# Decode attention on one core: weights loaded per head group, q projected in pairs, PV matmuls packed two rows at a time

## The chip, the cores and the metric

One core of one Trainium2 chip. The metric is the device time of one execution in microseconds (us). Each number for a version is the median of several executions. A ratio is computed from rounds in which two kernels ran on the same chip: the mean time of one kernel's runs over the mean time of the other's in the same rounds, so it is not quite the ratio of the medians quoted beside it.

## The reference, cut to what matters

Two attention blocks, each for one new token of two sequences, with 32 heads of 192 and a cache of 8192 keys and values per head. Everything is bf16.

```python
q = (x @ wq).reshape(B, 1, 32, 192).transpose(0, 2, 1, 3)      # B = 2, x is (2, 1, 640)
scores = einsum("bhqd,bhkd->bhqk", q, k_cache) * 192 ** -0.5    # k_cache (2, 32, 8192, 192)
p = softmax(scores, axis=-1)
o = einsum("bhqk,bhkd->bhqd", p, v_cache)
return o.transpose(0, 2, 1, 3).reshape(B, 1, 32 * 192) @ wo     # wo (6144, 640)
# two such blocks, A and B, side by side in the output: (2, 1, 1280)
```

2 blocks x 32 heads x 2 sequences make 128 units. A unit reads 3.1 MB of K and 3.1 MB of V; with one query per head, nothing is read twice.

## The kernel before: the parts that matter

In a unit u, K lies as 128 partitions x 64 rows x 192 (T = 64). VectorE multiplies K by q; for the first NA = 30 rows ScalarE sums the products (one ACTIVATE with an accumulator per row), for the other 34 VectorE adds them up. The row maximum mp is reduced over the partitions by GpSimd (`mg`), GpSimd multiplies it by minus the scale (`nb`), ScalarE takes exp with nb as bias, and PE multiplies the probabilities with V.

```python
K1 = min(cfg.get("K1", 6), NA - 1)       # accumulations of unit u ahead of exp of unit u-1
NV = cfg.get("NV", 3)                    # buffers for V; K has NK = 2

# SyncE, in this order: every transfer of a unit
for u in range(NU):
    if u % B == 0: sp_head_loads(u // B)                       # wq, wo of one head
    S_sp.add(sp_k(u), waits=[key("d1b", u - NK)])
    if u >= 1:
        S_sp.add(sp_v(u - 1), waits=[key("pv", u - 1 - NV)])

# GpSimd: for each unit an all-reduce over the partitions, then the small nb
for u in range(NU):
    S_pool.add(pool_ar(u), waits=[key("d3", u), key("nb", u - 2)], sig=("ar", u))
    S_pool.add(pool_nb(u), waits=[("ar", u), key("exp", u - 2)], sig=("nb", u))

# VectorE, slot u
d1a(u)      # prodA = K[:, 0:30] * q           waits for K, for a0 (q ready), for accumulations of u-2
d3(u - 1)   # mp = max of the scores of u-1    waits for the last accumulation of u-1
d1b(u)      # prodD = K[:, 30:64] * q
l1, l2, l3, r(u)   # sums of prodD
# f2 (reciprocal) in odd slots

# ScalarE, slot u
for t in range(K1): act_acc(u, t)
act_exp(u - 1)                                   # waits for nb(u-1)
# f1, f4 (evictions of PV) in odd slots
act_a0(u + 1)                                    # q of u+1 from PSUM
for t in range(K1, NA): act_acc(u, t)

# PE, unit u: 64 matmuls of 192 columns
for t in range(T):
    eng.matmul(ops[0:1, b, 0:Dh], pb[u % 2][:, t:t + 1], vb[u % NV][:, t, :], start=(t == 0), stop=False)
```

## Time and profile before

| | before |
|---|---|
| median | 3093.31 us at first, 3094.33 us with the 16 runs of the comparison |
| per unit | about 24.0 us |
| busy: PE, VectorE, ScalarE, GpSimd | 36%, 47%, 46%, 15% |
| transfers | 271 GB/s mean, 67.6% of the queues' time |
| nb to mp (ScalarE's part of the loop) | 9.48 us |
| mp to nb (GpSimd's part) | 14.54 us |

Such numbers are read like this: no engine and no queue is full, so some chain of waits sets the pace. The prediction shows the chain.

```profile
POOL mg L213 <- issue: 73.8, 7, 10.7
```

### The profile page before, as it was taken

The numbers are of one execution on the slowest core, as the hardware profiler recorded it, in microseconds if no ns is written. First come the engines' busy times: TensorE is split into PE (matmuls) and PEld (weight loads), VectorE is DVE, ScalarE is ACT, GpSimd is POOL, SyncE is SP. The second block draws the span as 40 slices with busy tenths as digits, with TensorE's granted clock in tenths as the row PEclk, the third lists the DMA queues.
The fourth block names the chain that finished last, engine by engine and source line by source line (L and its number), as shares of the span: only waits on it lengthen the run. The fifth ranks groups of instructions, "written<-read, shape, count | busy, mean of one in ns | idle before, by whom it ended". The sixth has DMA issues, their size and how long they took to land.

```text
span 3097.1 us, 31016 instructions
## 1 busy us (share of the span) xinstructions
PE 1128.4 (36%) x9856; PEld 952.3 (31%) x9856; DVE 1455.4 (47%) x960; ACT 1439.4 (46%) x8195; POOL 465.3 (15%) x266
## 2 busy tenths in 40 slices
PE   2334333433334333433333433343334333343334
PEld 1223322332223322332223322333223322333223
DVE  4444454444444454444544454445444454445443
ACT  4445544544445444444444544454444444454444
POOL 1111111111111111111111111111111111111111
PEclk8666666666666666666666666666666666666666
DMA  9677677766676667766677667766676666766661
GB/s 380 273 295 288 252 279 284 284 257 262 274 284 277 257 268 290 282 257 257 272 286 281 259 263 283 283 273 262 269 295 272 257 272 269 291 265 262 278 262 79
DMA packets 94964, 838.78 MB, mean 271 GB/s; under 512 B 49736, under 2 KB 62032, under 8 KB 62032
## 3 DMA queue, kind: packets, MB, share of 16 engines
q1 hardware_dynamic: 94784, 836.79, 67.6%
q8 instruction: 78, 1.28, 0.2%
q14 instruction: 86, 0.70, 0.1%
q10 hardware_dynamic: 16, 0.01, 0.0%
HBM read 836.77 MB, written 0.01 MB: 270 GB/s over the span
## 4 chain that ended last, share of the span: by engine, by line
issue 82%; POOL 15%; POOLq 1%; ACT 1%; DMA 0%; PE 0%; DVE 0%; SPq 0%
POOL mg L213 14%; POOL nb L218 1%; ACT prodA L278 1%; DMA kb<-in_A_k_cache_dram 0%; POOLq L218 0%; PE ops L354 0%; POOLq L401 0%; DVE prodD L235 0%; DVE prodA L230 0%; POOLq L213 0%; POOLq L46 0%; SPq L145 0%; SPq L151 0%; DVE s L244 0%; PE oTps L362 0%
## 5 line engine op out<-in xcount | busy, mean ns | idle before, releaser
L354 PE MATMUL ops<-vb,pb 128*1 128x192 bf16 x8192 | 971.6, 298 | 1944.4 <-ACT pb L284 989.4
L354 PEld LDWEIGHTS ops<-vb,pb 128*1 128x1 bf16 x8192 | 822.3, 102 | 2092.1 <-ACT pb L284 1004.4
L278 ACT ACTIVATE prodA<-prodA 128x192 bf16<-128x192 bf16 x3840 | 1326.0, 347 | 12.2 <-DVE prodA L230 11.3
L284 ACT ACTIVATE pb<-sc,nb 128x64 bf16<-128x64 f32 x128 | 44.5, 348 | 1624.2 <-POOL nb L218 1624.2
L278 ACT ACTIVATION_READ_ACCUMULATOR prodA<-prodA 128x1 f32 x3840 | 718.7, 187 | 0.0
L230 DVE TENSOR_TENSOR prodA<-kb,qbc 128x5760 bf16<-128x5760 bf16 x128 | 404.3, 3159 | 499.0 <-ACT qbc L296 481.7
L213 POOL PARTITION_ALL_REDUCE mg<-mp x128 | 428.8, 3350 | 1264.0 <-DVE mp L240 1180.2
L235 DVE TENSOR_TENSOR prodD<-kb,qbc 128x6528 bf16<-128x6528 bf16 x128 | 454.2, 3549 | 0.0
L240 DVE TENSOR_REDUCE mp<-sc 128x1 f32<-128x64 f32 x128 | 28.2, 220 | 644.6 <-ACT prodA L278 644.6
L244 DVE TENSOR_TENSOR s<-prodD 128x3264 bf16<-128x3264 bf16 x128 | 237.8, 1858 | 4.4
L218 POOL TENSOR_SCALAR nb<-mg 128x1 f32<-128x1 f32 x128 | 33.4, 261 | 1347.9 <-issue 1347.9
L258 DVE RECIPROCAL rc<-o_sb 1x2 f32<-1x2 f32 x64 | 9.8, 154 | 475.7 <-ACT o_sb L289 475.7
L247 DVE TENSOR_TENSOR s<-s 128x1632 bf16<-128x1632 bf16 x128 | 129.0, 1008 | 4.4
L254 DVE TENSOR_REDUCE sc<-s 128x34 f32<-128x816 bf16 x128 | 128.4, 1003 | 4.4
L345 PE MATMUL qps<-wqs,xbc 128*128 128x192 bf16 x640 | 76.2, 251 | 21.0 <-ACT qbc L296 12.8
L250 DVE TENSOR_TENSOR s<-s 128x816 bf16<-128x816 bf16 x128 | 74.6, 583 | 4.4
L345 PEld LDWEIGHTS qps<-wqs,xbc 128*128 128x128 bf16 x640 | 47.0, 98 | 39.7 <-issue 33.3
L362 PE MATMUL oTps<-rc,o_sb 1*96 1x1 f32 x512 | 53.4, 221 | 0.0
L362 PEld LDWEIGHTS oTps<-rc,o_sb 1*96 1x96 f32 x512 | 48.0, 159 | 2.4 <-issue 0.3
L372 PE MATMUL outps<-wos,oTz 96*4 96x320 bf16 x256 | 45.0, 297 | 0.9 <-ACT oTz L292 0.9
L296 ACT ACTIVATE qbc<-qps 128x192 bf16<-128x192 f32 x128 | 39.2, 306 | 7.2 <-PE qps L345 7.2
L289 ACT ACTIVATE o_sb<-ops 1x386 f32<-1x386 f32 x64 | 29.9, 466 | 9.1 <-PE oTps L362 9.1
(14 smaller groups left out, 102.0 us busy)
## 6 DMA issues: line engine op xcount, KB each, us to landing
kb<-in_A_k_cache_dram SPq DMA_DIRECT2D x64, 3072.0 KB, 10.2
vb<-in_A_v_cache_dram SPq DMA_DIRECT2D x64, 3072.0 KB, 17.3
kb<-in_B_k_cache_dram SPq DMA_DIRECT2D x64, 3072.0 KB, 10.3
vb<-in_B_v_cache_dram SPq DMA_DIRECT2D x64, 3072.0 KB, 17.3
wqs<-in_A_wq_dram SPq DMA_DIRECT2D x32, 240.0 KB, 3.2
wos<-in_A_wo_dram SPq DMA_DIRECT2D x32, 240.0 KB, 3.5
wqs<-in_B_wq_dram SPq DMA_DIRECT2D x32, 240.0 KB, 3.3
wos<-in_B_wo_dram SPq DMA_DIRECT2D x32, 240.0 KB, 3.5
```

Of the source, the lines that this page charges most:

```text
L213: return eng.partition_all_reduce(mg[u % 2][:], mp[u % 2][:], 128, bass.bass_isa.ReduceOp.max)
L218: return eng.tensor_scalar(nb[u % 2][:], mg[u % 2][:], -scale, None, ALU.mult)
L230: return eng.tensor_tensor(prodA[u % 2][:], kb[u % NK][:, 0:NA, :], qb_bc(u, NA), ALU.mult)
L235: return eng.tensor_tensor(prodD[:], kb[u % NK][:, NA:T, :], qb_bc(u, ND), ALU.mult)
L244: return eng.tensor_tensor(s1[:], prodD[:, :, 0:96], prodD[:, :, 96:192], ALU.add)
L247: return eng.tensor_tensor(s2[:], s1[:, :, 0:48], s1[:, :, 48:96], ALU.add)
L250: return eng.tensor_tensor(s3[:], s2[:, :, 0:24], s2[:, :, 24:48], ALU.add)
L254: return eng.tensor_reduce(sc[u % 2][:, NA:T], s3[:], AXL.X, ALU.add)
L278: return eng.activation(prodA[u % 2][:, t, :], prodA[u % 2][:, t, :], ACTF.Identity, accum_out=sc[u % 2][:, t:t + 1])
L345: ins = eng.matmul(qps[:, 0:Dh], xbc[blk][b][:, c, :], wqs[g % NWQ][:, c, :], start=(c == 0), stop=(c == DC - 1))
L354: eng.matmul(ops[0:1, b, 0:Dh], pb[u % 2][:, t:t + 1], vb[u % NV][:, t, :], start=(t == 0), stop=False)
L362: ins = eng.matmul(oTps[0:HP, 2 * c + b:2 * c + b + 1], o_sb[0:1, b, HP * c:HP * (c + 1)], rc[0:1, b, :], start=True, stop=True)
```

## The change

The intent: fewer, longer weight loads (four heads at once), one q projection for two heads, half as many PV matmuls with twice the columns, in-place additions that free memory, and the first use of the activation table moved to the start. With it come two numbers that the short description does not name: K1 from 6 to 18, and V's buffers from three to two.

```diff
-    K1 = min(cfg.get("K1", 6), NA - 1)
+    K1 = min(cfg.get("K1", 18), NA - 1)
-    NV = cfg.get("NV", 3)
+    NV = cfg.get("NV", 2)
+    HG = cfg.get("HG", 4)
 ...
-        pb = [sb(f"pb{i}", [128, T], BF16) for i in range(2)]
+        pb = [sb(f"pb{i}", [128, T // 2, 33], BF16) for i in range(2)]      # columns 0 and 32 used, rest 0
-        wqs = [sb(f"wqs{i}", [128, DC, Dh], BF16) for i in range(NWQ)]
-        wos = [sb(f"wos{i}", [HP, 2, D], BF16) for i in range(NWO)]
+        wqs = [sb(f"wqs{i}", [128, DC, HG * Dh], BF16) for i in range(2)]
+        wos = [sb(f"wos{i}", [HP, HG, 2, D], BF16) for i in range(2)]
 ...
-        for blk in range(NBLK):
-            for b in range(B):
-                S_sp.add(sp_x(blk, b))
+        for b in range(B):
+            S_sp.add(sp_x(0, b))
+        S_sp.add(sp_wq(0))
         for u in range(NU):
-            if u % B == 0:
-                sp_head_loads(u // B)
+            if u % UG == 0: ...                      # wq of the next group, wo of this one
             S_sp.add(sp_k(u), waits=[key("d1b", u - NK)])
             if u >= 1:
                 S_sp.add(sp_v(u - 1), waits=[key("pv", u - 1 - NV)])
+            if u == 1:
+                for blk in range(1, NBLK):
+                    for b in range(B):
+                        S_sp.add(sp_x(blk, b))
 ...
         def act_f1(eng):
-            return eng.activation(o_sb[:], ops[0:1, :, 0:Dh + 1], ACTF.Identity)
+            eng.activation(o_sb[0:1, :, :], ops[0:1, :, 0:Dh], ACTF.Identity)
+            eng.activation(o_sb[32:33, :, :], ops[32:33, :, Dh:2 * Dh], ACTF.Identity)
+            return eng.activation(lsb[:], ops[0:33, :, 2 * Dh:2 * Dh + 1], ACTF.Identity)
 ...
         def pe_pv(u):
-                for t in range(T):
-                    eng.matmul(ops[0:1, b, 0:Dh], pb[u % 2][:, t:t + 1], vb[u % NV][:, t, :],
-                               start=(t == 0), stop=False)
+                for j in range(T // 2):
+                    eng.matmul(ops[0:33, b, 0:QW], pb[u % 2][:, j, :], vv[:, j, :],     # QW = 384
+                               start=(j == 0), stop=False)
 ...   (a0 and p0 for two heads at once; additions of prodD in place; semaphores to match)
```

## The prediction

> **What bounds the kernel now.** I read the page's busy rows first, then the chain that ended last in order of time, then the waits, then the timeline of one period, and last the timeline of GpSimd at the very end, where the machine is otherwise empty. From the page:
>
> ```profile
> PE 1128.4 (36%) x9856; PEld 952.3 (31%) x9856; DVE 1455.4 (47%) x960; ACT 1439.4 (46%) x8195; POOL 465.3 (15%) x266
> ...
> q1 hardware_dynamic: 94784, 836.79, 67.6%
> ...
> L213 POOL PARTITION_ALL_REDUCE mg<-mp x128 | 428.8, 3350 | 1264.0 <-DVE mp L240 1180.2
> ```
>
> No engine is over half busy and the transfers take two thirds: the bound is a loop of waits. There are 128 units (2 blocks, 32 heads, 2 rows), so a unit takes 3093/128 = about 24 us. The chain that ended last, in order of time:
>
> ```profile
> 1506.32 0.26 POOL nb L218
> ...
> 1516.48 3.03 POOL mg L213
> 1519.51 0.07 POOLq L218 x2
> 1519.58 11.21 issue
> 1530.80 0.26 POOL nb L218
> ```
>
> Each unit it goes from one nb (the negated maximum that exp needs) to the next, 24.5 us here. The all-reduce is shown with 3 us, but nb, which waits for it, comes 14.3 us after its start: the 11.21 us of "issue" belong to it. The waits say who closes the loop:
>
> ```profile
> ACT pb L284 <- POOL nb L218: 1624.2, 128, 14.9
> ...
> POOL mg L213 <- DVE mp L240: 1180.2, 120, 23.7
> ...
> DVE mp L240 <- ACT prodA L278: 644.6, 127, 8.2
> DVE prodA L230 <- ACT qbc L296: 481.7, 125, 9.4
> ```
>
> Exp waits for nb, the all-reduce for the row maximum mp, mp for the last accumulation of ScalarE. The accumulations after exp are therefore on the loop. One period of the timeline (accumulations left out but the first):
>
> ```profile
> 1506.62 0.35 ACT L284 ACTIVATE pb<-sc,nb 128x64 bf16<-128x64 f32 x1 [12.16 <-POOL nb L218]
> ...
> 1506.96 0.31 ACT L296 ACTIVATE qbc<-qps 128x192 bf16<-128x192 f32 x1
> ...
> 1507.17 0.35 ACT L278 ACTIVATE prodA<-prodA 128x192 bf16<-128x192 bf16 x1
> ...
> 1507.37 3.16 DVE L230 TENSOR_TENSOR prodA<-kb,qbc 128x5760 bf16<-128x5760 bf16 x1 [6.69 <-ACT qbc L296]
> ...
> 1515.59 0.22 DVE L240 TENSOR_REDUCE mp<-sc 128x1 f32<-128x64 f32 x1 [5.05 <-ACT prodA L278]
> 1515.72 3.55 DVE L235 TENSOR_TENSOR prodD<-kb,qbc 128x6528 bf16<-128x6528 bf16 x1
> ...
> 1519.30 0.33 SPq L145 DMA_DIRECT2D kb<-in_B_k_cache_dram  x1
> ...
> 1522.86 1.00 DVE L254 TENSOR_REDUCE sc<-s 128x34 f32<-128x816 bf16 x1
> ```
>
> Accumulations start 0.344 us apart; 24 of the 30 follow exp (K1 = 6 go before it), from 1507.17 to 1515.4. From nb (1506.32) to mp (1515.59) is 9.27 us, and 9.69 in the odd units, which also have the evictions f1 and f4; mean over the run 9.475. From mp to the next nb the median over 120 middle units is 14.43, mean 14.54 (13.3 to 16.7). 9.475 + 14.54 = 24.01, and the nb are on average 24.01 us apart: these two terms are the whole loop. GpSimd at the end:
>
> ```profile
> 3053.40 3.57 POOL L213 PARTITION_ALL_REDUCE mg<-mp  x1 [9.37 <-DVE mp L240]
> 3064.25 0.26 POOL L218 TENSOR_SCALAR nb<-mg 128x1 f32<-128x1 f32 x1 [7.28 <-issue]
> 3074.08 0.38 POOL L213 PARTITION_ALL_REDUCE mg<-mp  x1 [9.57 <-DVE mp L240]
> 3081.87 0.26 POOL L218 TENSOR_SCALAR nb<-mg 128x1 f32<-128x1 f32 x1 [7.40 <-issue]
> ```
>
> The last all-reduce, with VectorE and transfers idle, needs 7.8 us to nb; the one before it, beside VectorE's products but without transfers, 10.85; in the middle it is 13 to 15.
>
> **What the Trainium skill says.** "SBUF — State Buffer", section "SBUF: two separate sides": VectorE instructions with two SBUF inputs and GpSimd instructions that read SBUF take a shared port pair exclusively, for a whole instruction. The trace agrees: the first part of the all-reduce is 3.57 us where the 3.55 us product runs beside it and 0.38 us where VectorE is idle. The same section says that DMA cannot slow an engine's access; the 3 to 4 us more of the middle units are then unexplained (the first unit has 10.9 with transfers at 407 GB/s), and I carry them along. "TensorE: Matmul & The Clock Gate", "Part 1: The HAM clock gate": a matmul costs N columns at 1.2 GHz cold or 2.4 GHz warm. The trace agrees in the main: with a granted clock of 0.50, 14 PV matmuls of 192 columns filled 1.80 us (129 ns; 192 columns at 1.2 GHz would be 160), with 1.00, 32 filled 2.40 us (75 ns; at 2.4 GHz 80), so the columns and the clock set PV's time, not the count of instructions. "ScalarE: Activation LUTs", "What ACT_TABLE_LOAD costs": ACTIVATEs cost a fixed part plus 0.833 ns per element; 192 more elements are an estimated 0.16 us by that page; f1's 386 elements took 0.37 us start to start here.
>
> **The change part by part.**
> 1. K1 goes from 6 to 18. The short description does not name it, but it is the only part in the middle of the loop. Twelve accumulations move from after exp to before it, into the time in which ScalarE waits for nb. On the path: 12 x 0.344 = 4.13 us less per unit. The 18 ahead of exp take 6.2 us from about mp on, inside the 14.5 of the all-reduce: hidden.
> 2. Paired q projections: a0 (qbc) runs in two of four units with 384 instead of 192 columns. 0.21 us per unit before, an estimated 0.4 in half of them after: zero on average. PE does the same columns. In the unit with neither a0 nor f2 ahead, one in four, the first product (3.16 us) no longer waits for exp; it runs right after the last reduction, 8 to 11.4 us after mp, inside the all-reduce. ScalarE takes it up no sooner.
> 3. PV two rows at a time: 32 matmuls of 384 columns replace 64 of 192. The columns are the same 12,288, so by the rates above PV stays near the 6.5 to 8.3 us that it takes now; the weight load count halves, but loads overlap matmuls. PV is not on the loop: exp two units later needs it. Gain 0.
> 4. f1 becomes three ACTIVATEs: two of 384 elements at 0.37 and a short one of about 0.1: 0.84 instead of 0.37 in odd units, +0.23 us per unit on average, on the path since accumulations follow it.
> 5. Weights in groups of four heads, longer runs per descriptor, K first, V with two buffers instead of three: no transfer ends a wait in the steady state (the only K wait among the waits is 17.2 us once). At the start K 0 now stands behind two wq groups and one wo group, 2.95 MB instead of 0.98: 1.97 MB at some 410 GB/s is +5 us, less what the short wq runs cost before. I put +4 us.
> 6. In-place additions on VectorE: same element counts, and off the loop: the last reduction ends 8.3 us after mp, 6 us before nb.
>
> Sum: nb to mp 9.475 - 4.13 + 0.23 = 5.58; plus 14.54 is 20.1 us per unit, 3.90 less. Times 127 gaps: 495 us. 3093 - 495 + 4 = 2602.
>
> **Does the shorter loop fit the rest?** ScalarE needs 30 x 0.344 plus about 1.5, some 12 us; VectorE the sum of its rows, about 11.4; PE about 9. The first product must end before the accumulations: nb + 1.2 + 3.2 = 4.4 against 5.1 in even units, 5.2 against 6.2 in odd ones: it fits with under 1 us. Transfers: 839 MB at the 420 to 440 GB/s of full stretches is about 1950 us, 75% of 2602. V of unit u is now issued after PV of u-2 (nb + 8.4), K of u+2 right after it (the second product ends at nb + 9.3). Their 6.29 MB take 15 us, so K lands some 5.5 us after the next nb, and its earliest reader, the free first product, comes at nb + 13.8. With a weight group (+1.97 MB, 4.7 us, every eighth unit) it still fits.
>
> **Rivals.**
> A: the all-reduce grows. In the free slot of part 2 a VectorE product lies in a part of the all-reduce that was clear of it. If it reads SBUF there again, up to 3.2 us in one unit of four: +0.8 per unit, 100 us, 2700. For it: the 3.57 against 0.38. Against it: the shared pair seems needed at its start only, since the second-last all-reduce, with VectorE busy up to 7.9 us after its start, lost 3.05 us, no more than the first product's length. The denser traffic could also lift it towards 15 to 15.5: +60 to 120 us.
> B: transfers become the bound through V's two buffers and the in-order queue, because V now stands before K and both wait. It would show as K waits on the first product, and a time of 2750 or more. Against it: the 8 us of slack above.
> C: the named parts (PV packing, fewer loads) carry the gain, or there is none. If PE mattered, PE would end a wait on the loop; it ends none in the list above. Then only K1 moves the time; without it the rest would be within 1% of before, some 2 to 3% off at most.
>
> **Range and chances.** I take 2602 plus a little for rival A, 2615. The range 2550 to 2700 holds an all-reduce term between 14.1 and 15.3. The 4.13 us are counted instructions, so faster by over 2% is nearly sure: 0.97; within 2% 0.02; slower 0.01.
>
> **What would show it.** Right: nb to mp about 5.2 us in even and 6.2 in odd units; mp to nb near 14.5; nb about 20 us apart; exp still waiting for nb, with about 8 us each instead of 12.7; PV 6.5 to 8.3 us per unit in 32 pieces; DMA share near 75 to 80%. Wrong: mp to nb over 15.5 (A), VectorE's first product waiting for K (B), mp waiting for something other than ScalarE, or PE ahead of exp (C).

## More of the kernel before

```profile
L213 POOLq MODIFY_POOL_CONFIG  x256: 11/11/11, 8.2 to 3064.9; - x128
```

In 7 of 128 units the all-reduce did not wait for mp but for something in GpSimd itself that had taken up to 10.7 us. And GpSimd's queue holds two configuration instructions for each all-reduce (and two for each nb).

## The result, and the profile after

The changed kernel runs at 2705.86 us median (2684.34 to 2729.79, 11 runs) against 3094.33; the ratio is 0.8739, 95% interval 0.8715 to 0.8764. It is 12.6% faster, but about 90 us slower than the forecast and just outside its range. Executions over 1.5% slower than the fastest of the same kernel are left out of the means.

The page of the changed kernel, the lines that answer to those of before:

```profile
PE 1110.0 (41%) x5440; PEld 603.1 (22%) x5440; DVE 1451.8 (54%) x962; ACT 1478.6 (55%) x8261; POOL 259.0 (10%) x267
...
q1 hardware_dynamic: 56384, 836.79, 77.0%
...
L364 PE MATMUL ops<-vb,pb 128*33 128x384 bf16 x4096 | 952.1, 408 | 1591.0 <-ACT pb L278 805.6
...
L220 POOL PARTITION_ALL_REDUCE mg<-mp x128 | 218.3, 1705 | 1033.7 <-issue 660.2
```

PV's busy time is 952 us against 972 before, although it has half the instructions. The surprise is in the last line: the all-reduce's shown time fell from 3350 to 1705 ns, and what it waits for is no longer mp but "issue". The waits say the same:

```profile
ACT pb L278 <- POOL nb L225: 1196.1, 128, 15.7
...
POOL mg L220 <- issue: 660.2, 82, 11.2
...
DVE mp L243 <- ACT prodA L274: 380.9, 127, 14.6
```

What happened 7 times before happens 82 times now. The chain that ended last, in order of time (start us, us, what), shows one such unit:

```profile
1514.43 0.27 POOL nb L225
...
1520.81 0.22 DVE mp L243
1521.03 3.48 DVE prodD L240
1524.50 1.41 issue
1525.91 0.72 POOL mg L220
1526.63 0.07 POOLq L225 x2
1526.70 12.41 issue
1539.11 0.26 POOL nb L225
```

The maximum mp is there at 1521.03, nothing else is missing, and still the all-reduce starts only at 1525.91, 11.5 us after the last nb. Right behind it GpSimd's queue runs the two configuration instructions that belong to the next nb (L225), and then 12.4 us pass before that nb.

From the timeline of all 128 units (means over units 4 to 123):

| us | before | after |
|---|---|---|
| nb to mp | 9.48 | 5.65 |
| mp to nb | 14.54 | 15.21 (11.1 to 21.0) |
| sum: one unit | 24.01 | 20.86 |
| mp to start of the all-reduce | 0.56 | 2.77 |
| start of the all-reduce to nb | 13.98 | 12.43 |
| nb to start of the next all-reduce | 10.04 | 8.41 (6.15 to 12.28) |
| first nb after the start | 42.6 | 57.4 |

The theory this led to, called T below: GpSimd reloads its instruction library twice per unit, once before the all-reduce and once before nb. The built program has 256 such reload instructions, in turn to library 1 for the all-reduce and back to library 0 for nb. The Trainium skill knows the cost: "GPSIMD Engine Reference", section 2.1 "Instruction dispatch", says that the first call to a freshly loaded kernel pays an instruction-memory load of about 6 us, with no visible instruction in the profile. The shortest time from nb to the next all-reduce here is 6.15 us, which agrees. Before the change, the first reload lay beside the 9.5 us from nb to mp and was nearly hidden. With 5.65 us it sticks out. The rivals: the all-reduce itself grows under the denser transfers, or the parts that the description names carry the gain.

### The profile page after: what moved, and what is told of

It is laid out like the page before. It is cut to its first block, busy times and chain, and to the rows that moved or that the text cites. A ratio compares the mean times of both kernels' runs of the same rounds, so it can differ in the third digit from the quotient of the medians.

```text
span 2712.8 us, 21983 instructions
## 1 busy us (share of the span) xinstructions
PE 1110.0 (41%) x5440; PEld 603.1 (22%) x5440; DVE 1451.8 (54%) x962; ACT 1478.6 (55%) x8261; POOL 259.0 (10%) x267
## 2 busy tenths in 40 slices
DMA packets 56529, 838.20 MB, mean 309 GB/s; under 512 B 7240, under 2 KB 17488, under 8 KB 23632
## 4 chain that ended last, share of the span: by engine, by line
issue 76%; POOL 9%; ACT 7%; DVE 6%; POOLq 1%; DMA 1%; PE 0%; SPq 0%
POOL mg L220 8%; ACT prodA L274 6%; DVE prodD L240 5%; POOL nb L225 1%; DMA kb<-in_A_k_cache_dram 1%; ACT pb L278 1%; DVE prodD L246 1%; POOLq L225 0%; DVE mp L243 0%; POOLq L420 0%; PE ops L364 0%; DVE prodA L237 0%; ACT o_sb L283 0%; ACT qbc L290 0%; ACT o_sb L282 0%
## 5 line engine op out<-in xcount | busy, mean ns | idle before, releaser
L364 PE MATMUL ops<-vb,pb 128*33 128x384 bf16 x4096 | 952.1, 408 | 1591.0 <-ACT pb L278 805.6
L364 PEld LDWEIGHTS ops<-vb,pb 128*33 128x33 bf16 x4096 | 481.3, 120 | 2050.8 <-ACT pb L278 829.4
L246 DVE TENSOR_TENSOR prodD<-prodD 128x3264 bf16<-128x3264 bf16 (+2 forms) x384 | 442.2, 1151 | 13.3
L220 POOL PARTITION_ALL_REDUCE mg<-mp x128 | 218.3, 1705 | 1033.7 <-issue 660.2
L225 POOL TENSOR_SCALAR nb<-mg 128x1 f32<-128x1 f32 x128 | 33.4, 261 | 1370.0 <-issue 1370.0
L249 DVE TENSOR_REDUCE sc<-prodD 128x34 f32<-128x816 bf16 x128 | 128.4, 1003 | 4.4
L353 PE MATMUL qps<-wqs,xbc 128*128 128x384 bf16 x320 | 64.7, 334 | 7.8 <-DMA wqs<-in_A_wq_dram 7.3
L373 PE MATMUL oTps<-rc,o_sb 33*96 33x1 f32 x512 | 56.0, 227 | 0.0
L373 PEld LDWEIGHTS oTps<-rc,o_sb 33*96 33x96 f32 x512 | 50.5, 165 | 1.2 <-issue 0.3
L282 ACT ACTIVATE o_sb<-ops 1x384 f32<-1x384 f32 x64 | 29.7, 463 | 7.8 <-PE oTps L373 7.8
L290 ACT ACTIVATE qbc<-qps 128x384 bf16<-128x384 f32 x64 | 30.2, 472 | 6.6 <-PE qps L353 6.6
L283 ACT ACTIVATE o_sb<-ops 1x384 f32<-1x384 f32 x64 | 30.9, 482 | 0.8
```

The lines of the kernel that those rows point to most:

```text
L220: return eng.partition_all_reduce(mg[u % 2][:], mp[u % 2][:], 128, bass.bass_isa.ReduceOp.max)
L225: return eng.tensor_scalar(nb[u % 2][:], mg[u % 2][:], -scale, None, ALU.mult)
L246: return lambda eng: eng.tensor_tensor(prodD[:, :, 0:w], prodD[:, :, 0:w], prodD[:, :, w:2 * w], ALU.add)
L249: return lambda eng: eng.tensor_reduce(sc[u % 2][:, NA:T], prodD[:, :, 0:24], AXL.X, ALU.add)
L353: ins = eng.matmul(qps[:, 0:QW], xbc[blk][b][:, c, :], wqs[w % 2][:, c, off:off + QW], start=(c == 0), stop=(c == DC - 1))
L364: eng.matmul(ops[0:33, b, 0:QW], pb[u % 2][:, j, :], vv[:, j, :], start=(j == 0), stop=False)
```

## The experiments

Twelve kernels ran. All were correct except the light-transfer one. Its output is wrong, which doesn't matter for the time.

**K1 alone.** The kernel before with one number changed.

```diff
-    K1 = min(cfg.get("K1", 6), NA - 1)
+    K1 = min(cfg.get("K1", 18), NA - 1)
```

> The kernel before with one number changed, K1 from 6 to 18; nothing else of the change. Theory T (what the trace of the changed kernel suggests): GpSimd reloads its instruction library before each all-reduce and before each nb, and a reload that was hidden while ScalarE accumulated now delays the all-reduce. Then nb to mp falls by 4.13 us to 5.35, mp to nb rises from 14.5 to about 15.2, the start stays near 43 us: about 2660 us. If the all-reduce term were constant (my prediction): 3094 - 127 x 4.13 = 2570 us. If the named parts (PV packing, paired projections, grouped weights) carry the gain: about 3094, no change.

Measured: 2621.72 us, ratio to before 0.8453 (0.8418 to 0.8488). K1 alone gives more than the whole change. The time lies between the 2570 us of the constant term and the 2660 of T. nb to mp fell to 5.33 us as both had it; mp to nb was 14.79, not the constant of my prediction and not the 15.2 of T, but with a pattern: 17.1 in even and 12.5 in odd units, where weights of one head are loaded every second unit. The wait from mp to the start of the all-reduce was 3.85 us, against 0.56 at K1 = 6, so the late GpSimd is not a matter of the other parts.

**All but K1.** The changed kernel with K1 back at 6.

```diff
-    K1 = min(cfg.get("K1", 18), NA - 1)
+    K1 = min(cfg.get("K1", 6), NA - 1)
```

> The changed kernel with K1 put back to 6: the named parts alone. If K1 carries the whole gain: nb to mp about 9.8 us (9.5 plus 0.2 to 0.3 for the longer eviction f1), mp to nb back to about 14.5 with the all-reduce starting within 0.6 us of mp, the start some 10 to 15 us later than before: 3120 to 3150 us, within 2% of before. If the named parts carry it: about 2700 to 2800 us.

Measured: 3249.91 us, ratio 1.0483 (1.0444 to 1.0521). The direction was expected, the size was not: everything else together costs 4.8%. nb to mp was 9.79 (+0.31, the longer f1), the all-reduce started 0.36 us after mp (T: the first reload is hidden again), but all-reduce to nb rose to 14.97. So the named parts do not carry the gain, and something among them lengthens the way from the all-reduce to nb.

**The start.** All x loaded first, as before the change; the two copies of block 1 then no longer hold GpSimd up.

```diff
-        for b in range(B):
-            S_sp.add(sp_x(0, b))
+        for blk in range(NBLK):
+            for b in range(B):
+                S_sp.add(sp_x(blk, b))
         S_sp.add(sp_wq(0))
 ...
-            if u == 1:      # x of block 1: removed here
```

> The changed kernel with the x of both blocks loaded first, as before, so that GpSimd's copies for block 1 no longer hold up the first all-reduce. If the late start (first nb at 57.4 us instead of 42.6) is due to that: first nb at 44 to 48 us and 10 to 13 us less in all, about 2694 us against 2706. If the start is late because K 0 stands behind more weights: first nb still about 55 us and no change.

Measured: first nb at 48.4 us instead of 57.4, so 9 of the 15 us of late start are due to the copies that waited for x of block 1, whose 2.5 KB stand behind K 1 and V 0. In the changed kernel they end at 42.1 us, though the first mp is there at 35.6, and another 6.4 us pass before the first all-reduce. The other 6 us remain and fit K 0 standing behind more weights; no run tests that. The whole time was 2701.41 us, ratio 0.8708 (0.8679 to 0.8737). That interval overlaps the changed kernel's, so the 9 us are shown in the trace but not in the total.

**nb on ScalarE.** GpSimd then runs nothing but all-reduces; in the built program one reload instruction is left, before the first.

```diff
-            S_pool.add(pool_nb(u), waits=[("ar", u), key("exp", u - 2)], sig=("nb", u))
+        def act_nb(u):
+            return lambda eng: eng.activation(nb[u % 2][:], mg[u % 2][:], ACTF.Identity, scale=-scale)
 ...
+                S_act.add(act_nb(u - 1), waits=[("ar", u - 1), key("exp", u - 3)], sig=("nb", u - 1))
                 S_act.add(act_exp(u - 1), ...
```

> The changed kernel with nb (the multiplication of the maximum by minus the scale) moved from GpSimd to ScalarE, right ahead of exp. GpSimd then runs nothing but all-reduces, and the built program loads its library once instead of 256 times. Theory T: both reloads leave the loop; mp to exp falls from 15.2 us to under 8, the loop term from 20.9 to 12 or 14 us, and then the transfers set the pace at some 15 to 16.5 us per unit: 1950 to 2150 us. Rival: the all-reduce itself takes 11 to 14 us and is stretched by the denser transfers; then only nb's own 0.3 to 0.6 us per unit goes: 2630 to 2690 us.

Measured: 2085.75 us, ratio 0.6729 (0.6707 to 0.6751). Its view of the all-reduce's source line, its queue and its waits:

```profile
L220 POOLq MODIFY_POOL_CONFIG  x2: 6/6/6, 42.5 to 42.5; - x2
```

```profile
q1 hardware_dynamic: 56384, 836.79, 97.9%
```

```profile
POOL mg L220 <- DVE mp L242: 1572.5, 127, 21.6
...
DVE prodA L236 <- DMA kb<-in_A_k_cache_dram: 290.6, 59, 15.7
...
DVE prodA L236 <- DMA kb<-in_B_k_cache_dram: 273.8, 56, 13.7
```

The configuration runs once, GpSimd waits for mp again in 127 of 128 units, and VectorE now waits for K: the transfers are full. In the timeline one unit has mp at 1011.66, the all-reduce at 1011.97 and nb on ScalarE at 1018.01: 6.35 us from mp to nb, of which 3.58 is the all-reduce's shown time beside VectorE's product. The rest is not GpSimd's. ScalarE has K1 = 18 accumulations ahead of nb in its order, and they fill 1011.78 to 1018.01; it waited for the all-reduce in only 2 of 128 units:

```profile
ACT nb L277 <- POOL mg L220: 1.9, 2, 1.2
```

So 15.2 - 6.35 = 8.9 us is less than what the alternation cost. The edit takes away nb's own 0.26 us and a hand-over on GpSimd as well, but the 8.9 us are far larger than these. The rival that the all-reduce itself takes 11 to 14 us has fallen, and T fits. What is shown is that the alternation of all-reduce and nb on GpSimd costs the time. That it is the reload of the library is inferred, from the 256 reloads that became one and from their gaps; no run kept a second GpSimd instruction without a reload. The one reload that is left shows no 6 us: its configuration runs at 42.5 us and the all-reduce starts at 42.57. Perhaps the library was still loaded from the execution before; that was not tested.

**nb on ScalarE in the kernel before.** The same edit, K1 still 6, nothing of the change.

> The kernel before (K1 still 6, none of the change) with only nb moved from GpSimd to ScalarE. Theory T (library reloads): mp to nb falls to the 6.35 us seen where the same was done in the changed kernel; with 9.5 to 9.7 us from nb to mp the loop is about 16 us, close to the transfers' 15 to 16: 2040 to 2130 us, within 2% of the changed kernel with the same edit. If the reloads matter only together with K1 = 18: 2500 us or more.

Measured: 2132.05 us, ratio 0.6883 (0.6862 to 0.6905). It came out 2 us above the expected range: 2.3% behind the changed kernel with the same edit, by the two ratios. mp to nb was not the expected 6.35 us but 3.92, the same in every unit to 0.01 us: with 6 accumulations ahead of nb, ScalarE waits for the all-reduce in every unit.

```profile
ACT nb L282 <- POOL mg L213: 205.9, 128, 1.6
```

This is GpSimd's part without the alternation, and 14.54 - 3.92 = 10.6 us is what the alternation cost in the kernel before. The queue is at 98.3% here too, at 393 GB/s mean instead of 402. The short weight runs (49,736 packets under 512 bytes against 7,240) and the longer loop (K1 = 6) are both candidates for those 2.3%; no run separates them. The trace speaks for the transfers: 402 / 393 is 2.3%, VectorE waits for K in 125 units, and nb to mp is 12.6 us here (10.7 at least) where the loop needs 9.48.

**Transfers nearly idle.** The changed kernel: from the fifth unit on K and V are loaded by 2 of 64 rows.

```diff
-            return dma(kb[u % NK][:], src, ksem[u % NK])
+            n = T if u < 4 else 2
+            return dma(kb[u % NK][:, 0:n, :], src[:, 0:n, :], ksem[u % NK])      # V alike
```

> The changed kernel, wrong on purpose: from the fifth unit on K and V are loaded by 2 of 64 rows only, so that the transfers are nearly idle; all instructions stay. If the bulk transfers stretch the reloads: nb to the all-reduce's earliest start about 6.2 us (the shortest seen), all-reduce to nb 7.7 to 10.9 us as at the end of the kernel before, where nothing was transferred; mp to nb about 11 us instead of 15.2, 17 us per unit, about 2200 us. If the reload takes its time whatever the traffic: mp to nb stays near 15 and the time near 2700.

Measured: 2248.58 us, ratio 0.726. mp to nb 11.39 us, nb to the next all-reduce 6.44 (6.01 to 7.19), all-reduce to nb 10.62. The transfers' traffic therefore lengthens GpSimd's part by 15.21 - 11.39 = 3.8 us per unit: 3.25 of it between the end of the all-reduce and nb (10.72 against 7.47 us), 0.55 in a later end of the all-reduce. Two units of its GpSimd timeline:

```profile
1505.92 3.57 POOL L222 PARTITION_ALL_REDUCE mg<-mp  x1 [6.10 <-DVE mp L245]
1516.82 0.26 POOL L227 TENSOR_SCALAR nb<-mg 128x1 f32<-128x1 f32 x1 [7.33 <-issue]
1522.83 2.82 POOL L222 PARTITION_ALL_REDUCE mg<-mp  x1 [5.75 <-DVE mp L245]
1533.36 0.26 POOL L227 TENSOR_SCALAR nb<-mg 128x1 f32<-128x1 f32 x1 [7.71 <-issue]
```

This is what reloads cost with hardly any traffic: here 7.3 and 7.7 us between the end of the all-reduce and nb, some 6 between nb and the next all-reduce. The weights are still loaded whole in this run. In the one unit in eight in which they are in flight, the first of these gaps is 9.2 us on average, in the others 7.2.

**Three V buffers at K1 = 6.** The run with all but K1, and NV back at 3.

```diff
-    NV = cfg.get("NV", 2)
+    NV = cfg.get("NV", 3)
```

> The changed kernel with K1 = 6 and V in three buffers again, so that V no longer waits for the PV of two units earlier and K and V are issued together after the second product, as in the kernel before. The run with K1 = 6 and two buffers had 14.97 us from the all-reduce to nb, the kernel before 13.98. If the earlier and separate V transfer, which now meets the reload from its start, causes that: back to about 14.0, 24.2 us per unit, some 3110 to 3150 us. If another named part causes it (longer f1 counted apart at 0.3 us): no change, 3250.

Measured: 3098.95 us, ratio 1.0005 (0.9972 to 1.0039), a little better than expected. The whole 4.8% came from the missing third buffer: mp to nb is 14.08 us instead of 15.33. With two buffers V waits for an earlier PV and its transfer starts some 1.3 us before the all-reduce; with three, K and V are issued together, 3.7 and 4.1 us after mp, as in the kernel before. The named parts without the buffer change are worth nothing either way at K1 = 6.

**Three V buffers at K1 = 18, and the reverse.** First the changed kernel with only NV back at 3.

> The changed kernel as it is (K1 = 18) with one number put back: V in three buffers instead of two. With K1 = 6 that gave back the whole 150 us. If the two V buffers are also what the changed kernel loses against the kernel before with K1 = 18 alone (2622 us): mp to nb falls from 15.2 to 14.2 to 14.8 us and the time from 2706 to between 2600 and 2660. If the loss at K1 = 18 is of another kind (GpSimd's own turn of reloads already sets the pace): 2690 to 2710.

Measured: 2775.03 us, ratio 0.8927 (0.8889 to 0.8965). A miss: it is slower than the changed kernel, not faster; mp to nb 15.77, nb to the next all-reduce 9.02. Then the kernel before with K1 = 18 and two buffers:

> The reverse: the kernel before with K1 = 18 and V in two buffers, nothing else. If the two buffers cost what is missing: from 2622 us up to 2670 to 2720. If they cost only together with the other named parts: 2622 stays.

Measured: 2697.94 us, ratio 0.8702 (0.8678 to 0.8726), as expected: 76 us more than with three. So at K1 = 18 the same number costs 76 us in one kernel and gains 69 in the other. What V's buffers do may depend on when the transfers fall relative to the two reloads; no run shifts the transfers alone, so this is not shown. I have no rule that says which is better; only that the effect is there. Read the other way, the four runs say that the named parts cost 8 us at K1 = 18 with two buffers (2698 to 2706) and 153 us with three (2622 to 2775).

**Shorter packets.** In the changed kernel the seventh unit of every eight, when long weight loads are in the queue, has all-reduce to nb in 9.18 us on average, the others 12.4 to 14.0. K and V rows are single packets of 24 KB, weights have runs of 1.5 and 2.5 KB. So perhaps the reload waits behind long packets.

```diff
-            src = blocks[blk]["k"][b, h].rearrange("(p t) d -> p t d", p=128)
-            return dma(kb[u % NK][:], src, ksem[u % NK])
+            src = blocks[blk]["k"][b, h].rearrange("(a p t) d -> p a (t d)", a=8, p=128)
+            return dma(kb[u % NK][:].rearrange("p (a t) d -> p a (t d)", a=8), src, ksem[u % NK])   # V alike
```

> The changed kernel with K and V read in pieces of 3,072 bytes instead of rows of 24,576 (token order permuted alike in K and V, so the result is the same); bytes, buffers and order of issue are unchanged. In the changed kernel the reload was fast (all-reduce to nb 7.7 to 9.5 us) in the one unit in eight in which weights with short runs were in flight, and slow (11 to 15) with K and V, whose rows are one 24 KB packet each. If the reload waits behind long packets: all-reduce to nb 8 to 10.5 us in all units, some 17.5 to 18.5 us per unit, 2250 to 2400 us. If the traffic slows it by its bytes alone: no change, 2690 to 2720. If shorter packets only slow the transfers: above 2720.

> The kernel before (K1 = 6) with the same edit. If the reload waits behind long packets: mp to nb from 14.5 to about 11 us, 20.5 us per unit, 2600 to 2700 us, without any of the change. If bytes alone matter: 3080 to 3110.

Measured: 2653.48 us for the changed kernel, ratio to before 0.8568 (0.8536 to 0.86), and 2998.71 for the kernel before, 0.9702 (0.9678 to 0.9726). Both are faster, by 2 to 3%, and both far from what the idea foretold: all-reduce to nb was 12.16 and 13.04 us, against 12.43 and 13.98. Packet length is a small part of the 3.8 us at most. Traffic by its bytes alone had been foretold without any gain, so neither branch came true. The premise was also a misreading. In one such stretch the last packet of weights ends at 1669.4 us; the seventh unit's all-reduce starts at 1672.30, and only K and V are in flight until its nb at 1683.33, in all such units at 421 GB/s on average. The weights lie ahead of that all-reduce and in the unit before, whose 12.75 us are not short. Why the seventh unit is fast stays open.

**A candidate for the fastest.** nb on ScalarE, all x first, three V buffers.

> The changed kernel with nb on ScalarE, all x loaded first, and V in three buffers: a candidate for the fastest. With nb alone moved it was at 2086 us with the transfers 97.9% busy, so at most 2% of idle and some 10 us of the start are left: 2050 to 2090 us. If it is slower than 2086, V and K in another order cost more than the third buffer gives.

Measured: 2084.03 us, ratio 0.673 (0.6708 to 0.6751): the same as with nb moved alone. With the queues at 97.3% there is nothing left that buffers or the start could give. Both versions beat the kernel before by 33% and the changed kernel by about 23%.

## Why the prediction was wrong, and where it was right

- **Part 1 of the change, K1 = 18: right.** nb to mp was foretold at 5.58 us and is 5.65, and 5.33 with K1 alone. The number that the description leaves out is the whole gain: alone it gives ratio 0.8453, all else alone 1.0483.
- **Parts 2, 3, 4: right.** The paired projections, the packed PV and the longer f1 cost 0.31 us per unit of nb to mp against the 0.23 worked out: f1's two long ACTIVATEs took 0.48 and 0.49 us start to start, not 0.37. a0 went from 0.21 to 0.37 us, which is the 0.16 more that the prediction estimated from "ScalarE: Activation LUTs", "What ACT_TABLE_LOAD costs". PV takes 6.66 to 8.33 us per unit (median 7.37), against 6.71 to 8.34 (7.71). The prediction's 129 and 75 ns per PV matmul count matmuls already under way in the window; starts are 160 ns apart at clock 0.50 and 82 to 83 at 1.00, and 320 and 162 to 163 with twice the columns. The free first product (rival A's first half) did no harm: the units whose all-reduce it lies in have 15.03 us, below the mean of 15.21.
- **Rival C: right in direction, wrong in size.** The named parts carry no gain, but without K1 the time was to be within 1%, 2 to 3% off at most; it was 4.8% longer, because of V's buffers.
- **Failed: the term "plus 14.54" of the sum, taken as a constant.** The sum was 5.58 + 14.54 = 20.1; it measured 5.65 + 15.21 = 20.86. That is 0.74 us, times 127 some 94 us. The step behind it was the reading of the chain. I took GpSimd's time as one latency that starts at mp. In truth GpSimd has a loop of its own, nb, reload, all-reduce, reload, nb, and mp enters it in the middle. Cutting the other branch by 4.13 us uncovered the first reload: mp to the start of the all-reduce went from 0.56 to 2.77 us, +2.21. It did not cost the full 2.21, because a late all-reduce meets less of VectorE's product: start after mp plus shown duration is 3.93 us again and again (0.36 + 3.57, 1.51 + 2.42, 1.82 + 2.11). It ends 0.25 us after the product, whenever it began beside it, which agrees with the lock that the Trainium skill describes in "SBUF — State Buffer", "SBUF: two separate sides", and that the prediction cites. In the kernel before this was so in all 120 units, in the changed kernel in 85. In 29 others the reload held it back until the next two-input addition had begun, and it ended 5.82 us after mp, as in the unit of the chain above. The mean end thus moved from 3.93 to 4.48 us after mp, +0.55, and the second reload from there to nb from 10.61 to 10.72, +0.11. Together that is the term's growth of 0.67 to within rounding.
- **The profile had shown it.** "POOL mg L213 <- issue: 73.8, 7, 10.7" says that at 9.5 us the reload was already at its limit in 7 units. I did not count it as a bound, and I wrote the growth of the term as rival A's tail (60 to 120 us) with too little weight. That tail is the size that came, but by luck: it was put down to denser traffic, and the reason is the first reload. Of the signs of being wrong that the prediction named, none came: mp to nb stayed under 15.5 us.
- **Failed: part 5's start, +4 us.** It is +14.8. Six fit K 0 behind the weights, about as worked out; 9 are due to GpSimd's copies for block 1, which stand in order ahead of the first all-reduce. I had followed the transfers and not GpSimd's own order.
- **Part 5's claim that V's two buffers cost nothing: failed too.** No transfer ends a wait in the loop, as foretold. But the number of buffers changes GpSimd's part: 150 us at K1 = 6, and 76 us or -69 us at K1 = 18. That it does so by moving the transfers against the reloads is likely, not shown.
- **Adding up:** 2602 + 94 + 11 = 2707, against 2706 measured. The growth of the term alone gives 2696, still inside the range; the late start carried the time out of it. (The profiled runs, from which the 94 comes, differ by 384 us where 491 were foretold: 107 less, by the same account 105.)

What stays open: why the bulk transfers lengthen GpSimd's part by 3.8 us. That they do is shown (light transfers), packet length explains little of it, weights in flight lengthen it too (9.2 against 7.2 us in that run), and the reloads leave no bytes of their own in the list of queues (86 and 81 packets on the instruction queue q14, with 256 reloads and with one).

## What to carry to other kernels

When a loop of waits is the bound, every engine in it has a loop of its own: write down for each what it does between two of its turns, and how long, before calling a term constant. Here a wait "for issue" in 7 of 128 units was the first sign of the next bound. And look at what alternates on GpSimd: one 0.26 us multiplication between all-reduces cost 10.6 us per unit in the kernel before, and moving it to another engine was worth more than everything else tried here.

## What the Trainium skill lacked or had wrong

- "GPSIMD Engine Reference", 2.1 "Instruction dispatch", gives the load as a cost of the first call. Lacking: an ordinary instruction between two all-reduces makes it recur. Here there are 256 reloads; without the alternation mp to nb fell from 14.54 to 3.92 us. Its figure of about 6 us fits with idle transfers (nb to all-reduce 6.01 to 7.19 us), though the gap from the all-reduce's end to nb was 7.2 us there; beside K and V streams nb to all-reduce was up to 12.3 us, which no page says. The single reload of the run with nb on ScalarE showed no such wait (configuration at 42.5 us, all-reduce at 42.57).
- "SBUF — State Buffer", "SBUF: two separate sides", says that DMA and engine accesses cannot contend. As a statement on accesses no run contradicts it, but GpSimd's part of a unit is 3.8 us longer beside full transfers (15.21 against 11.39 us), so it must not be read as "transfers do not slow GpSimd's work".
